# The 1e-9 of a softmax, stored behind its probabilities and summed with them

## The chip, the cores and the metric

One core of a Trainium2 chip runs the kernel. The metric is the device time of one execution in microseconds (us). The kernel before takes 829.16 us, the median of three runs (829.06 to 829.52).

A core has five engines with a queue of instructions each, worked off in order: TensorE (PE in the profile; PEld is its loading of weights), VectorE (DVE), ScalarE (ACT), GpSimd (POOL) and SyncE (SP), which here issues nearly all DMAs. Semaphores order the engines among each other.

## The reference

A windowed attention feeds a gated network; all values are float32.

```python
# q, k, v: (8, 8, 576, 64); heads 0-3 see the last 32 positions,
# heads 4-7 every fourth of the last 128
scores = scale * np.matmul(q, k.transpose(0, 1, 3, 2))
scores = np.where(masks[None, :, :, :], scores, -1000000000.0)
scores = scores - np.max(scores, axis=-1, keepdims=True)
attn = np.exp(scores)
attn = attn / (np.sum(attn, axis=-1, keepdims=True) + 1e-09)
x = np.matmul(attn, v)      # -> 4608 tokens of 512 columns
h = x @ w_in                # 512 x 2048
g = h * (1.0 / (1.0 + np.exp(-1.702 * h)))
out = g @ w_out             # 2048 x 512
```

The change touches the 1e-9 of the division.

## The kernel before

**Attention.** Heads are taken in pairs, four pairs for each of the eight batches: 32 pairs, k = 0 to 31. The queries of a pair lie on the 128 partitions in `QT` = 5 tiles for each of the two heads, and each query has a window of `W` = 64 keys, so the probabilities of a pair are a tile `pr` of 128 x (2 x 5 x 64), 640 columns. For each pair these steps follow one another:

- TensorE makes the scores in PSUM (L470 for the mask, where it is added by a product, and L482). From pair 8 on VectorE adds the mask as it copies them to `pr` (`add_mask`).
- `exponentials`: VectorE takes the maximum of each query (L502), subtracts it (L349), and ScalarE takes the exponential in place (L506).
- `softmax`: VectorE sums the 64 probabilities of each query into `sm`, 128 x 10 (L520). `inverse` adds 1e-9 to the ten sums (L510) and takes the reciprocal (L512). GpSimd, or VectorE, multiplies each head's probabilities by it (L349).
- VectorE transposes blocks of 32 x 32 into `ct` (L529 for the first four pairs, L533 for the others). From pair 4 on, eight copies carry the blocks into `bt` (DMAs for pairs 4 to 7, ScalarE or VectorE after that). TensorE multiplies with v (L575, L607), and `drain_x` copies the result out of PSUM; the copies of the last 64 tokens of a batch (its rests) are steps of their own.

The pairs use two sets of `pr`, `mx`, `sm`, `ct` in turn; pairs 8 to 23 use three. The third `pr` and `ct` lie in units 13 to 15 of a large tile `arena` (`third`), where the q, k and v of pair 3 have lain. Pair 8 is the first that uses it.

**The network.** The weights come as float32 and are split into a high and a low part (`decode`), and each product is the sum of three. Three groups of 512 tokens are done plainly (`Group`, L848 up and L785 to L789 down, `acc_m`). Six more groups are done in blocks p, q, r of two, with seven sums and differences in place of eight products (`Block`, L991 and L1106). While the first weights come in, the four first pairs run alone: this head lasts until about 38 us. Their drains feed the first group's products. The gate (L856, L857 or L1012, L1013) lies between the up and the down products. The attention of later batches is done beside the products of earlier groups. In the head, TensorE also runs products without use (L1237, `idle`).

**The order of the work** is not written out by hand. Each step is handed to `add` with the engines that may do it and its cost in us on each, an urgency, and the names that it reads and writes. A negative cost marks a VectorE step that holds the port which it shares with GpSimd. `Plan.ordered` places all steps one by one, four times over, with the costs as durations, and the queues are then filled in that order. A step that names what another writes comes after it in the plan. So whatever changes a cost or a name can move other steps too, on every engine, and the number of `idle` products as well.

Of the kernel before, what the change touches and what calls it, by code (L numbers as in the profile page):

```python
# [7 lines left out]
F32 = mybir.dt.float32  # L8
F32R = mybir.dt.float32r
AX = mybir.AxisListType  # L10
AF = mybir.ActivationFunctionType
ALU = mybir.AluOpType
# [5 lines left out]
P = 128  # L18
NC = DM // P
NF = DF // P  # L20
GT = 512
# [12 lines left out]
QT = 5  # L34
W = 64
# [7 lines left out]
PE, ACT, DVE, POOL, DMA = range(5)  # L43
# [4 lines left out]
class Plan:  # L48
# [9 lines left out]
    def add(self, costs, urgency, work, reads=(), writes=(), slack=0.0, count=0):  # L58

        i, after = len(self.ops), set()
        for k in reads:
            after.add(self.writer.get(k))
        for k in writes:  # L70
            after.add(self.writer.get(k))
            after.update(self.readers.get(k, ()))
        for k in writes:
            self.writer[k], self.readers[k] = i, []
        for k in reads:
            if k not in writes:
                self.readers.setdefault(k, []).append(i)
        self.ops.append((costs, (urgency, i), work, after - {None, i}, slack, count))
# [138 lines left out]
def tile_windowed_attention_then_gated_mlp(  # L217
# [10 lines left out]
    V, A, G, T = nc.vector, nc.scalar, nc.gpsimd, nc.tensor  # L228
# [8 lines left out]
    add = plan.add  # L237

    def fixed(shape, dt, name):
        return one.tile(shape, dt, tag=name, name=name)  # L240
# [25 lines left out]
    def area(first, n):  # L266
        return arena[:, first:first + n].rearrange("p u n -> p (u n)")
# [13 lines left out]
    sums_o = dram.tile([7 * PAIRS // 2, P, 2 * DM], F32, tag="sums_o", name="sums_o")  # L281
    tokens_x = dram.tile([B * NC, P, GT], F32, tag="tokens_x", name="tokens_x")
    tokens_r = dram.tile([NC, P, B * LT], F32, tag="tokens_r", name="tokens_r")
    prs = [fixed([P, 2, QT, W], F32, f"pr{j}") for j in range(2)]
    mxs = [fixed([P, 2, QT], F32, f"mx{j}") for j in range(3)]
    sms = [fixed([P, 2, QT], F32, f"sm{j}") for j in range(3)]

    cts = [fixed([P, 2, QT, 2, 32], F32, f"ct{j}") for j in range(2)]

    third = area(13, 3)  # L290
    prs.append(third[:, 0:2 * QT * W].rearrange("p (a t w) -> p a t w", a=2, t=QT))
    cts.append(third[:, 2 * QT * W:4 * QT * W].rearrange("p (h t a q) -> p h t a q", h=2, a=2, t=QT))

    four = tc.tile_pool(name="four", bufs=1, space=bass.MemoryType.PSUM)
    first_x = four.__enter__().tile([P, NC, GT], F32, tag="x", name="first_x")
# [9 lines left out]
    ident = fixed([P, P], BF16, "ident")  # L305
    ones = fixed([P, 32], F32, "ones")
    V.memset(ones, 1.0)
    V.memset(ident, 1.0)
    G.affine_select(out=ident, in_=ident, pattern=[[1, P]], compare_op=ALU.is_equal, fill=0.0, base=0,
                    channel_multiplier=-1)  # L310
# [37 lines left out]
    def pair(e, dst, a, b, op):  # L348
        (V if e == DVE else G).tensor_tensor(out=dst, in0=a, in1=b, op=op)  # L349
# [103 lines left out]
    def dilated(k):  # L453
        return k % NC >= NC // 2

    def turn(k):
        return k % (3 if FIRST * NC <= k < INNER else 2)

    def masked(k):

        return k < FIRST * NC
# [31 lines left out]
    def exponentials(k, urgency):  # L493
        u, y = pairs[k], turn(k)
        pr, mx = prs[y], mxs[y]
        PR, MX = f"pr{y}", f"mx{y}"
        held = ("sp",) if masked(k) else ()

        def sp():
            return u["all"] if masked(k) else pr  # L500

        add({DVE: 0.80}, urgency, lambda e: V.tensor_reduce(out=mx, in_=sp(), axis=AX.X, op=ALU.max),  # L502
            held or (PR,), (MX,))
        add({DVE: 0.80 if masked(k) else -0.80}, urgency, lambda e: pair(
            e, pr, sp(), mx[:, :, :, None].broadcast_to([P, 2, QT, W]), ALU.subtract), (*held, MX), (PR,))
        add({ACT: 0.75}, urgency, lambda e: A.activation(prs[y], prs[y], AF.Exp, scale=0.125), (), (PR,))  # L506

    def inverse(k, urgency):
        sm, SM = sms[turn(k)], f"sm{turn(k)}"
        add({DVE: -0.15}, urgency, lambda e: V.tensor_scalar(  # L510
            out=sm, in0=sm, scalar1=1.0e-9, scalar2=None, op0=ALU.add), (), (SM,))
        add({DVE: 0.19}, urgency, lambda e: V.reciprocal(out=sm, in_=sm), (), (SM,))  # L512

    def softmax(k, urgency):

        y = turn(k)
        pr, sm, ct = prs[y], sms[y], cts[y]
        PR, SM, CT = (f"{n}{y}" for n in ("pr", "sm", "ct"))
        exponentials(k, urgency)
        add({DVE: 0.80}, urgency, lambda e: V.tensor_reduce(out=sm, in_=pr, axis=AX.X, op=ALU.add), (PR,), (SM,))  # L520
        inverse(k, urgency)
        for a in range(2):
            add({POOL: 0.85, DVE: -0.48}, urgency, lambda e, a=a: pair(
                e, pr[:, a], pr[:, a], sm[:, a, :, None].broadcast_to([P, QT, W]), ALU.mult), (SM,), (f"{PR}.{a}",))
        if k < NC:

            for a in range(2):
                to = ct.rearrange("p h t a q -> p (h t a q)")[:, a * QT * W:a * QT * W + QT * W]
                add({DVE: 0.48}, urgency, lambda e, a=a, to=to: V.transpose(  # L529
                    out=to, in_=pr[:, a].rearrange("p t w -> p (t w)")), (PR, f"{PR}.{a}"), (f"{CT}.{a}",))  # L530
            return
        for half in (0, 1):
            add({DVE: 0.42}, urgency, lambda e, half=half: V.transpose(  # L533
                out=ct[:, half].rearrange("p t a q -> p a t q"), in_=pr[:, :, :, 32 - 32 * half:64 - 32 * half]),
                (PR, f"{PR}.0", f"{PR}.1"), (f"{CT}.{half}",))

        for m in range(8):
            j, prev = m % 4, m // 4  # L540
            odd, upper = j % 2, j // 2
            row = D * upper + 32 * (odd != prev)
            col = 32 * odd if not prev or odd else 64
            shift = prev and not odd
            tiles = slice(1 if shift and not upper else 0, QT - upper)
            to = slice(1, QT) if upper and not shift else slice(0, tiles.stop - tiles.start)
            dst = bt[row:row + 32, to, :, col:col + 32]
            src = ct[32 * j:32 * j + 32, prev, tiles]

            def work(e, dst=dst, src=src):  # L550
                if e == DMA:
                    load(dst, src)
                else:
                    copy(e, dst, src)

            costs = {DMA: 82} if k < FIRST * NC else {ACT: 0.49, DVE: -0.33}
            add(costs, urgency, work, (f"{CT}.{prev}",), (f"bt.{m}",))
# [134 lines left out]
    def attention(k, urgency):  # L692

        def alone(j):
            add({PE: 1.6 if masked(j) else 1.1}, urgency - 1.0e5, lambda e: scores(j),
                (lots(j)[0], *(["mask"] if dilated(j) else [])), ("sp", "left", f"scores{j}"), 1.0)
            if not masked(j):
                add_mask(j, urgency)

        n = following(k)  # L700
        if k == NC:
            load_qk(k)
            alone(k)
        load_v(k)
        if n and n > k + 1:
            if k == FIRST * NC:
                for j in range(k + 1, n):
                    load_qk(j)
                    alone(j)
            load_qk(n)  # L710
        elif n and k != INNER:
            load_qk(n)
        softmax(k, urgency)
        joint = n is not None and n > k + 1
        if n and not joint and k != INNER:
            alone(n)

        def work(e):
            if joint:
                scores(n)  # L720
            product(k)

        need = [lots(n)[0] if joint else f"scores{n}"] if n else []
        places = ("sp",) if k >= INNER else ("left", "av", "sp") if joint else ("left", "av")
        add({PE: 1.95 if joint else 1.05}, urgency - 1.0e5, work,
            (lots(k)[1], *(f"bt.{m}" for m in range(8)), *need), places, 1.0)
        if joint:
            add_mask(n, urgency)
        drain_x(k, urgency)
# [9 lines left out]
    def unit(i):  # L739
        if i < NU:  # L740
            return arena[:, i]
        if i >= NU + 4:
            n = i - NU - 4
            if n < 4:
                tag = ("qk", "v")[n // 2]
                if f"{tag}_units" not in misc:
                    misc[f"{tag}_units"] = temp([P, 2, GT], F32, tag, f"{tag}_units")
                return misc[f"{tag}_units"][:, n % 2]
            if n >= 8:
                return bt_all[:, GT * (n - 8):GT * (n - 7)]  # L750
            if n < 6:
                return prs[n - 4].rearrange("p a t w -> p (a t w)")[:, 0:GT]
            return cts[n - 6].rearrange("p h t a q -> p (h t a q)")[:, 0:GT]
        if "wi_last" not in misc:
            misc["wi_last"] = temp([P, 4, GT], F32, "wi_last", "wi_last_units")
        return misc["wi_last"][:, i - NU]
# [535 lines left out]
```

## Time and profile before

| | |
|---|---|
| median of 3 runs | 829.16 us |
| profiled execution | 828.89 us |
| its span, from the first to the last instruction | 827.2 us |
| mean granted clock of TensorE | 0.991 |
| TensorE busy | 811.2 us |
| VectorE busy | 669.7 us |
| ScalarE busy | 515.0 us |
| GpSimd busy | 327.8 us |

The profile shows one execution. A row of a group of instructions gives line, engine, operation, what is written and read, the shapes and the count, then the busy time in us and the mean of one in ns, then how long the engine stood idle just before them and on what it waited. A row of the chain gives a start and a duration in us: the chain is followed back from the last instruction, at each step to what released it. A row of the order in time gives start, duration, engine and line, and in brackets an idle time before it. Durations of neighbours overlap a little, because an instruction's end is written down after the next one has begun. `L349` and `L342` are helpers, so their tiles tell which step they are.

### The profile page before, as it was taken

What the parts mean: (1) busy time and instruction counts of PE and PEld (TensorE: products, weight loads), DVE (VectorE), ACT (ScalarE), POOL (GpSimd) and SP (SyncE); (2) the same over time, 40 slices, a digit from 0 to 9 for tenths busy, and PEclk for the clock granted to TensorE, in tenths of its full rate; (3) what the DMA queues carried; (4) which work ended last, traced back from release to release, by engine and by line L of the source; (5) the groups of instructions that cost most, each with busy time, mean ns of one, the idle gap of its engine ahead of it and who ended that gap; (6) DMA issues with size and microseconds to landing.
All of it is one profiled execution on the core that took longest, in us unless ns stands there. A gap on an engine that the chain in (4) does not pass through costs nothing.

```text
span 827.2 us, 18837 instructions
## 1 busy us (share of the span) xinstructions
PE 811.2 (98%) x7240; PEld 653.5 (79%) x7240; DVE 669.7 (81%) x1104; ACT 515.0 (62%) x992; POOL 327.8 (40%) x296
## 2 busy tenths in 40 slices
PE   7899999999999999999999999999999999999997
PEld 4678777888878888878788788888888888888886
DVE  6898989787888778898989998977679876867575
ACT  7998986676676777586776655446446544544340
POOL 3343336566655663324235357331125431112251
PEclk8799999999999999999999999999999999999999
DMA  9476658889757567868878878675665658664546
GB/s 359 152 244 193 181 192 287 295 281 314 249 189 254 183 200 257 267 190 280 279 229 261 261 233 260 219 269 168 214 193 182 211 186 273 203 222 149 189 151 181
DMA packets 109610, 188.12 MB, mean 227 GB/s; under 512 B 26448, under 2 KB 55376, under 8 KB 109520
## 3 DMA queue, kind: packets, MB, share of 16 engines
q1 hardware_dynamic: 109376, 186.78, 69.3%
q8 instruction: 57, 0.93, 0.5%
q14 instruction: 33, 0.27, 0.1%
q10 hardware_dynamic: 144, 0.13, 0.0%
HBM read 140.64 MB, written 45.09 MB: 225 GB/s over the span
## 4 chain that ended last, share of the span: by engine, by line
PE 88%; DVE 7%; ACT 1%; issue 1%; DMA 1%; SPq 0%; DVEq 0%; ACTq 0%
PE hp_m L848 15%; PE up_q L991 9%; PE up_r L991 9%; PE up_p L991 8%; PE second_q_Q L1106 5%; PE second_r_Q L1106 5%; PE second_p_Q L1106 5%; PE acc_m L785 5%; PE acc_m L789 5%; PE acc_m L786 4%; PE sp L482 3%; PE second_r_Z L1106 3%; PE second_R L1106 3%; PE second_q_Z L1106 3%; PE second_p_Z L1106 2%; PE av L607 2%
## 5 line engine op out<-in xcount | busy, mean ns | idle before, releaser
L349 POOL TENSOR_TENSOR arena<-arena 128x256 f32<-128x256 f32 (+3 forms) x109 | 118.0, 1091 | 155.7 <-DVE wi_last_units L349 34.7
L848 PE MATMUL hp_m<-xs,wi_kept 128*128 128x512 f32 x504 | 129.1, 398 | 0.7 <-DVE xs L349 0.4
L848 PEld LDWEIGHTS hp_m<-xs,wi_kept 128*128 128x128 f32 x504 | 93.3, 188 | 22.5 <-DVE arena L857 1.6
L342 ACT ACTIVATE wo_kept<-arena 128x512 fp32r<-128x512 f32 x115 | 71.9, 629 | 42.3 <-PE second_r_Q L1106 11.4
L349 POOL TENSOR_TENSOR wo_kept<-arena,wo_kept 128x512 fp32r<-128x512 f32 x34 | 45.3, 1340 | 105.5 <-ACT wo_kept L342 72.2
L991 PE MATMUL up_p<-wi_kept,xs 128*128 128x512 f32 x336 | 84.7, 394 | 2.2 <-DVE arena L349 1.3
L991 PE MATMUL up_r<-wi_kept,xs 128*128 128x512 f32 x336 | 85.3, 389 | 0.0
L991 PE MATMUL up_q<-wi_kept,xs 128*128 128x512 f32 x336 | 83.4, 389 | 0.0
L991 PEld LDWEIGHTS up_p<-wi_kept,xs 128*128 128x128 f32 x336 | 62.1, 188 | 16.8 <-DVE arena L349 2.2
L991 PEld LDWEIGHTS up_q<-wi_kept,xs 128*128 128x128 f32 x336 | 63.0, 188 | 13.4 <-DVE arena L1013 0.3
L991 PEld LDWEIGHTS up_r<-wi_kept,xs 128*128 128x128 f32 x336 | 63.1, 188 | 13.1
L349 DVE TENSOR_TENSOR wo_kept<-arena,wo_kept 128x512 fp32r<-128x512 f32 x87 | 65.3, 761 | 5.9 <-ACT wo_kept L342 5.4
L349 POOL TENSOR_TENSOR wo_kept<-wi_last_units,wo_kept 128x512 fp32r<-128x512 f32 x23 | 31.9, 1388 | 84.6 <-ACT wo_kept L342 84.6
L785 PE MATMUL acc_m<-gh,wo_kept 128*128 128x512 f32 x156 | 61.7, 395 | 0.4 <-ACT arena L342 0.3
L786 PE MATMUL acc_m<-gh,wo_kept 128*128 128x512 f32 x156 | 60.9, 390 | 0.0
L349 POOL TENSOR_TENSOR pr<-pr,sm 128x320 f32<-128x320 f32 x52 | 43.3, 850 | 43.0 <-DVE sm L512 29.3
L342 ACT ACTIVATE bt<-ct 32x256 f32<-32x256 f32 (+1 forms) x127 | 55.2, 435 | 3.2 <-DVE ct L533 0.9
L1012 ACT ACTIVATE arena<-arena 128x512 f32<-128x512 f32 x60 | 37.5, 628 | 28.9 <-DVE arena L349 25.1
L349 DVE TENSOR_TENSOR gl<-arena,gh 128x512 fp32r<-128x512 f32 x53 | 44.9, 847 | 9.1 <-PE acc_m L789 6.4
L349 DVE TENSOR_TENSOR arena<-arena 128x512 f32<-128x512 f32 (+1 forms) x68 | 50.4, 747 | 0.4
L1013 DVE SCALAR_TENSOR_TENSOR arena<-arena 128x512 f32<-128x512 f32 x60 | 48.1, 807 | 0.7 <-ACT arena L1012 0.2
L342 ACT ACTIVATE wo_kept<-wi_last_units 128x512 fp32r<-128x512 f32 x47 | 29.6, 629 | 30.0 <-PE second_r_Z L1106 8.9
(261 smaller groups left out, 1826.6 us busy)
## 6 DMA issues: line engine op xcount, KB each, us to landing
xs<-sums SPq DMA_DIRECT2D x168, 256.0 KB, 3.3
out_weights<-sums_o SPq DMA_DIRECT2D x63, 512.0 KB, 3.8
qk<-qk_dram SPq DMA_DIRECT2D x29, 576.0 KB, 5.2
xs<-sums_o SPq DMA_DIRECT2D x21, 512.0 KB, 3.6
v<-vp_dram SPq DMA_DIRECT2D x28, 320.0 KB, 4.4
sums<-arena SPq DMA_DIRECT2D x32, 256.0 KB, 3.6
sums_o<-arena SPq DMA_DIRECT2D x32, 256.0 KB, 3.4
arena<-wi_dram SPq DMA_DIRECT2D x15, 512.0 KB, 4.7
```

Source lines behind the costliest of these rows:

```text
L342: A.activation(dst, src, AF.Copy, scale=scale)
L349: (V if e == DVE else G).tensor_tensor(out=dst, in0=a, in1=b, op=op)
L482: T.matmul(dst[:, w:w + n], u["qk"][rows, at:at + 32], u["qk"][rows, S + first:S + first + n], start=not masked(k), stop=True, tile_positi ...
L607: T.matmul(u["x"][i][rows, at:at + last - first], u["v"][keys, a, m], bt[keys, m, a, first:last], start=(bank_, a) not in begun, stop=True ...
L785: T.matmul(self.acc[j], w[:, 0, cols], high, start=f == 0, stop=False)
L786: T.matmul(self.acc[j], w[:, 1, cols], high, start=False, stop=False)
L789: T.matmul(self.acc[j], w[:, 0, P * j:P * j + P], low, start=False, stop=f == NF - 1)
L848: T.matmul(hps[f], wi(f)[:, st, cols], mv[:, c], start=c == 0 and k == 0, stop=c == NC - 1 and k == 2)
L991: T.matmul(self.banks[place], xs[:, slot, at:at + P], wi_kept[:, 2 * a + c, mv], start=fresh and c == 0 and k == 0, stop=c == 1 and k == 2 ...
L1012: add({ACT: 0.60}, -10.0, lambda e: A.activation(unit(tmp), src(), AF.Tanh, scale=0.851), need, own(tmp))
L1013: add({DVE: -0.70 if need[0][0] == "A" else 0.70}, -10.0, lambda e: V.scalar_tensor_tensor(out=unit(dst), in0=unit(tmp), scalar=1.0, in1=s ...
L1106: T.matmul(self.second[key], w[:, st, cols], mv, start=fresh and y == 0 and k == 0, stop=y == 1 and k == 2, skip_group_check=True)
```

## The change

Each `pr` becomes a set of 128 x (2 x 5 x 65): behind the 64 probabilities of a query stands one more column that holds 1e-9. The sum reads all 65, and the addition of L510 goes. The steps that work on probabilities use a view of the first 64 columns of each row, whose rows then begin 65 words apart. Two sets get their column by a memset ahead of the plan, on VectorE; the third gets it by a step of the plan, on VectorE or GpSimd, which names `pr2`, `first v3` and `first qk3`. The names `first v3` and `first qk3` are written by the loads of pair 3 and also by the rests of batch 1 (pairs 4 to 7). The third `ct` lies ten words further on.

```diff
-    prs = [fixed([P, 2, QT, W], F32, f"pr{j}") for j in range(2)]
+    sets = [fixed([P, 2, QT, W + 1], F32, f"pr{j}") for j in range(2)]
...
-    prs.append(third[:, 0:2 * QT * W].rearrange("p (a t w) -> p a t w", a=2, t=QT))
-    cts.append(third[:, 2 * QT * W:4 * QT * W].rearrange("p (h t a q) -> p h t a q", h=2, a=2, t=QT))
+    sets.append(third[:, 0:2 * QT * (W + 1)].rearrange("p (a t w) -> p a t w", a=2, t=QT))
+    prs = [p[:, :, :, 0:W] for p in sets]
+    cts.append(third[:, 2 * QT * (W + 1):2 * QT * (2 * W + 1)].rearrange("p (h t a q) -> p h t a q", h=2, a=2, t=QT))
...
     V.memset(ones, 1.0)
+    for p in sets[0:2]:
+        V.memset(p[:, :, :, W], 1.0e-9)
     V.memset(ident, 1.0)
...
     def inverse(k, urgency):
         sm, SM = sms[turn(k)], f"sm{turn(k)}"
-        add({DVE: -0.15}, urgency, lambda e: V.tensor_scalar(
-            out=sm, in0=sm, scalar1=1.0e-9, scalar2=None, op0=ALU.add), (), (SM,))
         add({DVE: 0.19}, urgency, lambda e: V.reciprocal(out=sm, in_=sm), (), (SM,))
...
-        add({DVE: 0.80}, urgency, lambda e: V.tensor_reduce(out=sm, in_=pr, axis=AX.X, op=ALU.add), (PR,), (SM,))
+        add({DVE: 0.81}, urgency, lambda e: V.tensor_reduce(out=sm, in_=sets[y], axis=AX.X, op=ALU.add), (PR,), (SM,))
...
                 add({DVE: 0.48}, urgency, lambda e, a=a, to=to: V.transpose(
-                    out=to, in_=pr[:, a].rearrange("p t w -> p (t w)")), (PR, f"{PR}.{a}"), (f"{CT}.{a}",))
+                    out=to.rearrange("p (t w) -> p t w", w=W), in_=pr[:, a]), (PR, f"{PR}.{a}"), (f"{CT}.{a}",))
...
             if k == FIRST * NC:
+                add({DVE: 0.10, POOL: 0.10}, urgency, lambda e: (V if e == DVE else G).memset(sets[2][:, :, :, W], 1.0e-9),
+                    (), ("pr2", "first v3", "first qk3"))
```

The blocks use the sets as plain storage once the attention is done; they take the first 512 columns of a set in place of a `pr`.

More of the change, by code (lines that the diff above doesn't have):

```diff
@@ L751, in unit @@
             if n < 6:
-                return prs[n - 4].rearrange("p a t w -> p (a t w)")[:, 0:GT]
+                return sets[n - 4].rearrange("p a t w -> p (a t w)")[:, 0:GT]
             return cts[n - 6].rearrange("p h t a q -> p (h t a q)")[:, 0:GT]
```

## The prediction

> **What bounds the kernel now.** I read the page first, then the stretches of the span, then the chain of work that ended last, then the groups of instructions with shapes kept apart, and last the order in time around the touched steps. The page:
>
> ```profile
> span 827.2 us, 18837 instructions
> PE 811.2 (98%) x7240; PEld 653.5 (79%) x7240; DVE 669.7 (81%) x1104; ACT 515.0 (62%) x992; POOL 327.8 (40%) x296
> PE 88%; DVE 7%; ACT 1%; issue 1%; DMA 1%; SPq 0%; DVEq 0%; ACTq 0%
> ```
>
> TensorE is busy for 98% of the span, and the chain lies on it for 88%. VectorE, the engine that the change relieves, carries 7% of the chain, some 58 us. The stretches say where a faster VectorE could matter (columns: busy time and instruction count of PE, PEld, DVE, ACT, POOL, then granted clock, DMA share, GB/s):
>
> ```profile
> 0.00:40.00 40.00, 32.12 (x844) 20.68 (x845) 29.32 (x67) 32.85 (x48) 14.90 (x23) 0.83 0.68 252
> ...
> 90.00:122.00 32.00, 31.91 (x352) 24.97 (x352) 28.61 (x50) 28.58 (x53) 11.03 (x9) 1.00 0.60 189
> 122.00:150.00 28.00, 27.56 (x360) 21.37 (x359) 24.90 (x44) 17.43 (x39) 18.89 (x19) 1.00 0.84 274
> 150.00:800.00 650.00, 647.16 (x5089) 528.24 (x5088) 525.12 (x844) 387.67 (x776) 257.78 (x226) 1.00 0.71 229
> 800.00:827.20 27.20, 22.41 (x99) 18.21 (x98) 16.28 (x26) 4.10 (x7) 7.08 (x5) 0.96 0.57 174
> ```
>
> TensorE stands idle for 7.88 us in the first 40 us (40.00 less 32.12), for 4.79 us after 800, and between 90 and 800 for only 0.09 + 0.44 + 2.84 = 3.37 us. The last reciprocal of a softmax starts at 451.7:
>
> ```profile
> L512 DVE RECIPROCAL sm<-sm x32: 198/210/219, 12.0 to 451.7; 128x10 f32<-128x10 f32 x32
> ```
>
> so the tail has none of this work. Whatever VectorE is spared, the middle can return at most 3.4 us, and the rest must come from the head.
>
> **The change part by part.** The times stand against the profiled execution, 828.89 us for a span of 827.2; the median of the timed runs is 829.16, 0.03% above it.
>
> *The removed addition.* There are 32 of them, one per pair of heads:
>
> ```profile
> L510 DVE TENSOR_SCALAR sm<-sm 128x10 f32<-128x10 f32 x32 | 7.9, 247 | 0.4
> L520 DVE TENSOR_REDUCE sm<-pr 128x10 f32<-128x640 f32 x26 | 21.0, 808 | 2.2 <-ACT pr L506 2.0
> L533 DVE STREAM_TRANSPOSE ct<-pr 128x320 f32<-128x320 f32 x44 | 20.5, 491 | 0.5 <-POOL pr L349 0.5
> ```
>
> They take 7.9 us of VectorE's 669.7, 1.2%. The chain of work says how much of that sets the end. It holds the addition three times:
>
> ```profile
> 9.83 0.82 DVE sm L520
> ...
> 11.24 0.09 DVE sm L510
> ...
> 133.20 0.08 DVE sm L510
> ...
> 141.94 0.17 DVE sm L510
> ...
> 167.96 0.73 DVE sm L520
> ```
>
> That is 0.09 + 0.08 + 0.17 = 0.34 us to win. The other 29 additions lie beside TensorE's work. The Trainium skill has its own price in "Perfetto Trace Analysis", section "Optimizing Scalar/DVE Operations": about 60 ns of engine time for each VectorE instruction on SBUF, and three of those would make 0.18 us in place of 0.34. The row's mean of 247 ns is four times that; I go by the chain.
>
> *The longer sum.* Each reduction reads 650 elements in place of 640. From the two rows above, an element costs (808 - 491) / (640 - 320) = 1.0 ns, as an estimate that takes both operations to be streams of the same rate; so each sum grows by 0.01 us, 0.3 us over all 32. The chain holds five sums between 9.83 and 167.96, so 0.05 us is lost.
>
> *The two memsets at the start* stand on VectorE between the one of the ones and the one of the identity:
>
> ```profile
> 0.88 0.09 DVE L307 MEMSET ones<- 128x32 f32 x1 [0.88 <-PEq L1282]
> 0.94 0.17 DVE L308 MEMSET ident<- 128x128 bf16 x1
> 4.22 0.69 PE L470 MATMUL sp<-plain,ident 128*128 128x320 bf16 x2 [1.64 <-DVE plain L328]
> 5.07 1.44 PE L482 MATMUL sp<-qk 64*32 64x64 f32 x84 [0.15 <-DMA qk<-qk_dram]
> ```
>
> One memset of this size holds the engine for 0.94 - 0.88 = 0.06 us, so the identity, GpSimd's selections behind it and the first mask come 0.12 us later. The first mask product at 4.22 waits for that, but the scores behind it wait another 0.15 us for q and k to land: 0.12 fits, so I take nothing. Without that cover it costs 0.12 us.
>
> *The reciprocal comes sooner.* With the addition gone, the reciprocal follows the sum, and the multiplication on GpSimd follows that. Where it could matter most is the last pair of the head (k = 3), whose product and split let the full-rate matmuls begin:
>
> ```profile
> 28.12 1.20 DVE L510 TENSOR_SCALAR sm<-sm 128x10 f32<-128x10 f32 x1
> 29.35 0.22 DVE L512 RECIPROCAL sm<-sm 128x10 f32<-128x10 f32 x1
> ...
> 31.80 0.27 DVE L344 COPY arena<-first_x 128x64 f32<-128x64 f32 x1 [1.68 <-ACT xs L342]
> 31.94 0.50 DVE L529 STREAM_TRANSPOSE ct<-pr 128x320 f32<-128x320 f32 x1
> ...
> 33.31 0.51 DVE L529 STREAM_TRANSPOSE ct<-pr 128x320 f32<-128x320 f32 x1
> ```
>
> ```profile
> 28.01 1.28 POOL L349 TENSOR_TENSOR wi_kept<-arena,wi_kept 128x512 fp32r<-128x512 f32 x1 [0.40 <-ACT wi_kept L342]
> 29.65 1.73 POOL L349 TENSOR_TENSOR pr<-pr,sm 128x320 f32<-128x320 f32 x2 [0.36 <-DVE sm L512]
> ```
>
> The addition took 1.20 us there where those of the chain above show 0.08 to 0.17: it stood until GpSimd's operation of 28.01 ended at 29.29. The reciprocal can start 1.23 us sooner, but GpSimd itself is taken until 29.29, so its multiplication gains 0.36 us. And in the present order the transposes stand behind the copy at 31.80, which waits for ScalarE and not for the softmax. So the gain is between 0 and 1.23 us; with the order unchanged it is 0, and I take that, because the copy's row has 1.68 us of waiting to swallow it.
>
> *The new wait.* The third set lies where the v and q, k of the pair k = 3 lay. Its memset, a planned step on VectorE or GpSimd, names "first v3", which the copies of the last 64 tokens of pair 7 write, and "pr2", which the maximum of pair 8 reads. So pair 8's maximum must now follow pair 7's drain, which it did not:
>
> ```profile
> 112.42 0.82 DVE L502 TENSOR_REDUCE mx<-arena 128x10 f32<-128x640 f32 x1
> ...
> 114.21 0.81 DVE L349 TENSOR_TENSOR arena<-arena,mx 128x640 f32<-128x640 f32 x1
> ...
> 122.68 0.42 DVE L398 TENSOR_SCALAR arena<-arena 128x512 uint32<-128x512 uint32 x1
> 123.91 0.69 DVE L857 SCALAR_TENSOR_TENSOR arena<-arena,hp_m 128x512 f32<-128x512 f32 x1 [0.81 <-ACT arena L856]
> 124.51 0.81 DVE L520 TENSOR_REDUCE sm<-arena 128x10 f32<-128x640 f32 x1
> ```
>
> ```profile
> 120.18 0.73 ACT L506 ACTIVATE arena<-arena 128x640 f32<-128x640 f32 x1
> ...
> 122.16 0.47 ACT L342 ACTIVATE arena<-sp 128x16 f32<-128x16 f32 x2
> ```
>
> ```profile
> 105.00:124.50 19.50, 19.50 (x192) 15.50 (x192) 15.45 (x28) 16.28 (x40) 7.45 (x7) 1.00 0.51 172
> 124.50:143.50 19.00, 18.56 (x215) 14.05 (x213) 18.15 (x32) 11.37 (x22) 11.48 (x11) 1.00 0.87 288
> ```
>
> The drain's two small copies end at 122.16 + 0.47 = 122.63. The maximum moves from 112.42 to 122.7 or later, the subtraction and the exponential after it: 0.82 + 0.81 = 1.63 us of VectorE leave a stretch with 4.05 us free (19.50 less 15.45) for one with 0.85 (19.00 less 18.15). If the memset stands on VectorE, the gate's operation at 123.91 is queued behind it, and TensorE's next products wait for that. Between nothing and 0.82 + 0.81 + 0.73 (exponential) + 0.10 (two of the memset rows) = 2.46 us. I take nothing: 0.81 us of idle before 123.91 holds the maximum, the 0.85 us hold the subtraction, and pair 8's rest (its addition is the one of the chain at 133.20, 8 us behind the sum of 124.51) is not in a hurry.
>
> *The order of everything else.* The steps' order is planned from costs, and 32 costs go, 32 change, one comes. What TensorE stands idle for in the middle, 3.37 us, bounds what a luckier order gives; I take as much for an unluckier one, and zero as the value, since nothing in the trace favours a side.
>
> Sum: 828.89 - 0.34 + 0.05 = **828.6 us**. The measurement of this kernel can tell about 0.2%, 1.66 us, from no change, so this is no change.
>
> **The rivals.** *The head gets shorter.* If the planner, free of the addition, puts pair 3's multiplication ahead of GpSimd's operation at 28.01 and its transposes ahead of the copy at 31.80, the whole 1.23 us is won: 828.6 - 1.23 = 827.4, faster by 0.2%; half of the middle's 3.37 us on top gives 825.7. For it: the 1.20 us of an operation over ten columns. Against it: the copy at 31.80.
>
> *Pair 8's wait reaches TensorE.* If VectorE stands at pair 8's sum until the late exponential is done, the gate's operations queue behind it and all 2.46 us count: 828.6 + 2.46 = 831.1, slower by 0.23%. It decides when 2.2 of the 2.46 us become TensorE's wait (830.8). For it: VectorE is busy for 18.15 of the 19.00 us into which the work moves. Against it: the 8 us that the softmax now waits behind its sum.
>
> *Rows of 65 words make each pass over the probabilities slower.* Every second row of 64 then begins on an odd word. Head pairs pass over them by maximum, subtraction and two transposes, 0.82 + 0.81 + 2 x 0.49 = 2.61 us; the other operations scale alike. If these lose a fifth, four head pairs cost 4 x 0.52 = 2.1 us and 32 pairs 16.7 us of VectorE, 8.8 more than the 7.9 removed, of which the chain's 7% is 0.6: 831.3. At a tenth it is 828.6 + 1.04 + 0.03 = 829.7, no change; the point is a sixth, 830.8. No row here has such a stride. The Trainium skill, "Vector Engine (DVE) Microarchitecture Reference", section 5.2, measures 1.30 ns in place of 1.054 per column for pairs of words that start odd; on half the rows that would be some 12% and a time of 830.0, an estimate from that page, which speaks of short pairs and not of runs of 64.
>
> *An unluckier order* costs up to 3.37 us: 832.0.
>
> **How the numbers follow.** The forecast gets 0.42, since the chain holds little of what goes. The shorter head gets 0.32: the head has the most idle time, and a planner with fewer steps to place there may well use it. Pair 8's wait gets 0.13 for its slack, odd rows 0.05, since a sixth is more than even the page's price, and an unluckier order 0.08. Hence faster 0.32, same 0.42, slower 0.26. The range reaches half-way into the outer cases: 825.8, next to the rival with a better middle, to 831.4, past pair 8's price and short of the unluckiest order.
>
> **What would show it.** The additions are gone, and sums take 0.01 us more each; memsets of 128x10 stand near 0.9 us and the first scores still start near 5.07. The maximum of pair 8 starts after 122 and TensorE's idle time from 122 to 150 stays near 0.44 us. The full-rate matmuls start within 0.3 us of now, where the chain shows them from 38.18 on:
>
> ```profile
> 38.18 3.92 PE hp_m L848 x16
> ```
>
>  VectorE's passes over the probabilities keep 0.81 us. The forecast is wrong if TensorE's idle time in the first 40 us falls by more than a microsecond, if that of 122 to 150 grows by as much, or if those passes grow.

## The result, and the profile after

The changed kernel takes 834.2 us, the median of six runs (832.22 to 835.32), against 829.14 us before (six runs, 828.83 to 829.65): a ratio of 1.0056, with a 95% interval from 1.0042 to 1.0070. It is slower, by 4.6 us in the means and 5.1 us in the medians, and outside the stated range of 825.8 to 831.4. The profiled execution took 833.98 us.

The page of the changed kernel shows nothing of this at first sight: the busy times of all engines stand within some 1% of those before. In the chain, DMAs carry 4% and not 1%, but e5 below, which is faster than before, has 4% as well.

```profile
span 832.2 us, 18826 instructions
PE 811.9 (98%) x7245; PEld 654.5 (79%) x7245; DVE 669.9 (80%) x1088; ACT 513.7 (62%) x982; POOL 323.7 (39%) x293
PE 85%; DVE 7%; DMA 4%; issue 1%; ACT 1%; SPq 0%; DVEq 0%; ACTq 0%
```

The stretches show where the 5.0 us of span came from. First the kernel before, with the stretch from 40 to 90 that the prediction left out and its long stretch cut in three, then the changed kernel (columns as there):

```profile
40.00:90.00 50.00, 50.00 (x503) 40.07 (x502) 45.46 (x79) 44.41 (x76) 18.11 (x15) 1.00 0.69 217
...
150.00:345.00 195.00, 194.72 (x2494) 157.72 (x2493) 161.03 (x283) 137.04 (x310) 105.67 (x111) 1.00 0.76 251
345.00:500.00 155.00, 152.75 (x1278) 123.23 (x1277) 138.18 (x228) 104.18 (x220) 58.67 (x49) 1.00 0.77 245
500.00:800.00 300.00, 299.68 (x1320) 247.29 (x1319) 225.90 (x335) 146.46 (x248) 93.44 (x67) 1.00 0.64 206
```

```profile
0.00:40.00 40.00, 31.02 (x840) 19.62 (x840) 28.87 (x61) 28.53 (x45) 16.34 (x24) 0.83 0.64 242
40.00:90.00 50.00, 47.73 (x461) 37.45 (x463) 45.65 (x82) 44.94 (x73) 13.23 (x13) 1.00 0.72 230
...
122.00:150.00 28.00, 27.58 (x296) 22.22 (x295) 25.45 (x41) 18.75 (x41) 17.32 (x16) 1.00 0.66 219
150.00:345.00 195.00, 194.12 (x2601) 157.70 (x2599) 157.15 (x273) 134.92 (x300) 107.03 (x114) 1.00 0.75 247
345.00:500.00 155.00, 153.42 (x1279) 123.29 (x1278) 138.86 (x224) 106.11 (x221) 60.51 (x48) 1.00 0.78 255
500.00:800.00 300.00, 298.58 (x1314) 245.98 (x1313) 230.02 (x335) 146.66 (x249) 90.24 (x64) 1.00 0.64 205
```

TensorE's idle time (length less busy time) went from 0.00 to 2.27 us between 40 and 90, from 0.28 to 0.88, from 2.25 to 1.58 and from 0.32 to 1.42 in the last three. Together that is 3.3 of the 5.0 us. The greatest piece lies right behind the head, where before there was none. In the first 40 us idle time is no measure of a loss, because TensorE also runs products without use there: it went from 7.88 to 8.98 us, but in e1 below, which takes the time of before, it is 9.40.

The work that is left tells how far a kernel has come. Behind 90 us TensorE is busy for another 811.16 - 32.12 - 50.00 = 729.04 us before, and for 811.90 - 31.02 - 47.73 = 733.15 us in the changed kernel. So 4.1 of the 5.0 us are lost by 90 us. This measure is rough: e1 and e3 below, whose orders are that of before until about 112 us, have 0.5 and 1.6 us more left than before.

The head itself ends later. The order in time on TensorE in the changed kernel, from the second part of the second head pair's product (k = 1, at 22.21) to the product of the last (k = 3, at 38.19):

```profile
22.21 1.61 PE L577 MATMUL first_x<-ct,arena 32*64 32x32 f32 x87 [2.21 <-issue]
23.75 0.71 PE L474 MATMUL sp<-arena,ident 128*128 128x320 bf16 x2
...
38.19 1.08 PE L577 MATMUL first_x<-ct,arena 32*64 32x64 f32 x80
39.20 5.08 PE L852 MATMUL hp_m<-xs,wi_kept 128*128 128x512 f32 x21
45.51 1.66 PE L852 MATMUL hp_m<-xs,wi_kept 128*128 128x512 f32 x6 [1.24 <-DVE arena L861]
47.01 0.39 PE L789 MATMUL acc_m<-gh,wo_kept 128*128 128x512 f32 x1
```

and before:

```profile
19.62 0.71 PE L470 MATMUL sp<-arena,ident 128*128 128x320 bf16 x2 [0.23 <-DVE pr L349]
...
34.00 1.08 PE L575 MATMUL first_x<-ct,arena 32*64 32x64 f32 x80
...
38.18 3.92 PE L848 MATMUL hp_m<-xs,wi_kept 128*128 128x512 f32 x16 [0.43 <-DVE xs L349]
41.94 0.39 PE L785 MATMUL acc_m<-gh,wo_kept 128*128 128x512 f32 x1
```

Before, the last pair's scores (their mask product) start at 19.62, ahead of the second pair's product; now they start at 23.75, behind it, and that product had stood still for 2.21 us in the middle ("issue": nothing that the profile shows held it). The last pair's own product starts at 38.19 and not at 34.00, and the first down product (`acc_m`) at 47.01 and not at 41.94. Not all of those 5.1 us are lost, since more up products stand ahead of it.

On VectorE the two orders part before that. The changed kernel, with one row of GpSimd at its head:

```profile
10.51 1.28 POOL L353 TENSOR_TENSOR wi_kept<-arena,wi_kept 128x512 fp32r<-128x512 f32 x1 [5.51 <-ACT wi_kept L346]
...
9.94 0.83 DVE L522 TENSOR_REDUCE sm<-pr 128x10 f32<-128x650 f32 x1 [0.20 <-ACT pr L510]
10.81 0.22 DVE L514 RECIPROCAL sm<-sm 128x10 f32<-128x10 f32 x1
10.94 0.76 DVE L506 TENSOR_REDUCE mx<-sp 128x10 f32<-128x640 f32 x1
11.94 1.12 DVE L394 TENSOR_SCALAR arena<-arena 128x512 uint16<-128x512 uint16 x1 [0.23 <-ACT arena L399]
12.87 0.84 DVE L353 TENSOR_TENSOR pr<-sp,mx 128x640 f32<-128x640 f32 x1
```

and before:

```profile
10.56 0.68 DVE L349 TENSOR_TENSOR wi_kept<-arena,wi_kept 128x512 fp32r<-128x512 f32 x1
11.16 0.17 DVE L510 TENSOR_SCALAR sm<-sm 128x10 f32<-128x10 f32 x1
11.24 0.82 DVE L502 TENSOR_REDUCE mx<-sp 128x10 f32<-128x640 f32 x1
11.97 0.21 DVE L512 RECIPROCAL sm<-sm 128x10 f32<-128x10 f32 x1
12.09 0.82 DVE L349 TENSOR_TENSOR pr<-sp,mx 128x640 f32<-128x640 f32 x1
```

The first reciprocal does come sooner, at 10.81 in place of 11.97, and the second pair's maximum too. That is the new order and not the missing addition: a step of the weights' decoding (`wi_kept`, 0.68 us at 10.56) has gone from VectorE to GpSimd, and in e1, without the addition and in the old order, the first reciprocal starts at 11.94. The planner then puts another step of the decoding (L394, 1.12 us and an idle 0.23) ahead of the second pair's subtraction, which so moves from 12.09 to 12.87. From there the orders differ throughout the head; which of the differences makes the last pair late was not separated.

### The profile page after: what moved, and what is told of

Its sections match the earlier page's. It is cut to its first block, busy times and chain, and to the rows that moved or that the text cites. A ratio compares the mean times of both kernels' runs of the same rounds, so it can differ in the third digit from the quotient of the medians.

```text
span 832.2 us, 18826 instructions
## 1 busy us (share of the span) xinstructions
PE 811.9 (98%) x7245; PEld 654.5 (79%) x7245; DVE 669.9 (80%) x1088; ACT 513.7 (62%) x982; POOL 323.7 (39%) x293
## 4 chain that ended last, share of the span: by engine, by line
PE 85%; DVE 7%; DMA 4%; issue 1%; ACT 1%; SPq 0%; DVEq 0%; ACTq 0%
PE hp_m L852 15%; PE up_r L995 9%; PE up_p L995 8%; PE up_q L995 7%; PE second_q_Q L1110 5%; PE second_r_Q L1110 5%; PE acc_m L793 5%; PE acc_m L789 5%; PE acc_m L790 5%; PE second_p_Q L1110 3%; PE sp L486 3%; PE second_r_Z L1110 3%; PE second_q_Z L1110 3%; PE second_R L1110 3%; PE av L609 2%; PE second_p_Z L1110 2%
## 5 line engine op out<-in xcount | busy, mean ns | idle before, releaser
L353 POOL TENSOR_TENSOR arena<-arena 128x256 f32<-128x256 f32 (+3 forms) x102 | 108.4, 1077 | 151.0 <-ACT arena L346 29.0
L353 POOL TENSOR_TENSOR wo_kept<-arena,wo_kept 128x512 fp32r<-128x512 f32 x36 | 49.3, 1376 | 113.9 <-ACT wo_kept L346 91.0
L353 DVE TENSOR_TENSOR wo_kept<-arena,wo_kept 128x512 fp32r<-128x512 f32 x85 | 67.0, 797 | 5.6 <-ACT wo_kept L346 5.0
L353 DVE TENSOR_TENSOR arena<-arena 128x512 f32<-128x512 f32 (+1 forms) x71 | 54.5, 772 | 1.6 <-ACT arena L346 1.0
L353 DVE TENSOR_TENSOR gl<-arena,gh 128x512 fp32r<-128x512 f32 x53 | 40.4, 761 | 9.3 <-PE acc_m L793 6.1
L860 ACT ACTIVATE arena<-hp_m 128x512 f32<-128x512 f32 x48 | 28.7, 599 | 29.0 <-PE hp_m L852 20.7
```

Source lines behind the costliest of these rows:

```text
L860: add({ACT: 0.60}, -10.0, lambda e: A.activation(g32, hps[f], AF.Tanh, scale=0.851), (place,), ("g32",))
```

## The experiments

Each ratio is to executions of the kernel before that were made beside the experiment. "Order" is the order in which the planner fills the queues of instructions; the planner also chooses the engine of a step that several may do, so a new order can also move work from one engine to another.

**e1: the new instructions in the old order.** Against the changed kernel:

```diff
+        add({DVE: -0.15}, urgency, lambda e: None, (), (SM,))
         add({DVE: 0.19}, urgency, lambda e: V.reciprocal(out=sm, in_=sm), (), (SM,))
...
-        add({DVE: 0.81}, urgency, lambda e: V.tensor_reduce(out=sm, in_=sets[y], ...
+        add({DVE: 0.80}, urgency, lambda e: V.tensor_reduce(out=sm, in_=sets[y], ...
...
-                add({DVE: 0.10, POOL: 0.10}, urgency, lambda e: (V if e == DVE else G).memset(...
+            if k == FIRST * NC:
+                V.memset(sets[2][:, :, :, W], 1.0e-9)
```

The empty step keeps the planned cost of the addition that is gone; the third memset is issued inside the step of pair 8's maximum and has none of its own.

> The change's instructions in the order of before: 65 columns, no addition, three memsets, while the planner still counts a step of 0.15 us for each addition (which issues nothing), 0.80 us for the sum, and no step for the third memset, which is issued with the maximum of pair 8. Theory A, that the loss is the new order of the steps: 828 to 829.5 us, no slower than before, as the prediction's sum had it. Theory B, that the instructions themselves cost it (rows 65 words apart, the memsets at the start, the longer sums): 832 to 835 us.

Measured: 828.97 us, ratio 0.9996 (0.9987 to 1.0005). In its trace VectorE, ScalarE and GpSimd run the steps of before in the sequence of before, the additions and memsets aside. Theory B falls: the 65 columns, the memsets, the longer sums and the missing addition come to nothing together, within -1.1 and +0.4 us.

**e2: the old instructions in the new order.** Against the kernel before:

```diff
-        add({DVE: -0.15}, urgency, lambda e: V.tensor_scalar(
-            out=sm, in0=sm, scalar1=1.0e-9, scalar2=None, op0=ALU.add), (), (SM,))
-        add({DVE: 0.19}, urgency, lambda e: V.reciprocal(out=sm, in_=sm), (), (SM,))
+        def both(e):
+            V.tensor_scalar(out=sm, in0=sm, scalar1=1.0e-9, scalar2=None, op0=ALU.add)
+            V.reciprocal(out=sm, in_=sm)
+
+        add({DVE: 0.19}, urgency, both, (), (SM,))
```

with 0.81 for the sum and an empty step for the third memset.

> The instructions of before, the additions among them, in the order that the changed kernel's planner makes: the addition is issued together with the reciprocal behind it, the sum is planned with 0.81 us, and a step that issues nothing stands for the third memset. Theory A (order): 833 to 835.5 us. Theory B (instructions): 828.5 to 830 us.

Measured: 833.38 us, ratio 1.0043 (1.0028 to 1.0057). The loss comes with the order, without one new instruction: VectorE, ScalarE and GpSimd run their steps in the sequence of the changed kernel, the additions and memsets aside. Its stretches have the mark of the changed kernel, idle time between 40 and 90:

```profile
0.00:40.00 40.00, 31.12 (x844) 19.11 (x845) 30.59 (x63) 29.38 (x45) 16.80 (x24) 0.91 0.65 242
40.00:90.00 50.00, 48.06 (x490) 37.42 (x489) 46.05 (x87) 45.69 (x73) 13.74 (x13) 1.00 0.73 227
```

while e1 has that of the kernel before:

```profile
40.00:90.00 50.00, 50.00 (x503) 40.05 (x502) 45.19 (x76) 44.35 (x73) 18.11 (x15) 1.00 0.70 222
```

**e3: only the third memset's step is new in the plan**; the addition's 0.15 and the sum's 0.80 are counted as in e1.

> The changed kernel, but the planner counts the addition's 0.15 us and 0.80 us for the sum as before, so its order is that of before until pair 8, where the third memset's step with its three names makes the maximum of pair 8 wait for pair 7's drain. Theory A with the loss in the head: 828 to 830 us, the head as before. Theory C, that pair 8's wait costs most of it: 831 us or more, with TensorE idle for over 2 us between 122 and 150.

Measured: 835.03 us, ratio 1.0071 (1.0054 to 1.0089), the slowest of all. This was not expected by the theory that puts the loss in the head: the head is that of before. Theory C has the time right, past its 831 us, but not the place. TensorE is idle for 1.91 us between 122 and 150, a little less than its 2 us and 1.5 more than before. More comes later, in stretches with other work: 0.8, 0.9 and 1.2 us more idle time than before between 150 and 345, 345 and 500, and 500 and 800. The first and the last two of these stretches:

```profile
122.00:150.00 28.00, 26.09 (x357) 20.49 (x354) 24.07 (x39) 16.08 (x35) 15.61 (x17) 1.00 0.81 273
...
345.00:500.00 155.00, 151.84 (x1265) 121.88 (x1264) 135.90 (x214) 107.16 (x224) 61.16 (x46) 0.99 0.76 241
500.00:800.00 300.00, 298.46 (x1316) 246.63 (x1315) 226.66 (x334) 145.77 (x247) 92.12 (x65) 1.00 0.64 206
```

**e4: the kernel before, with the sum planned as 0.81 in place of 0.80.**

```diff
-        add({DVE: 0.80}, urgency, lambda e: V.tensor_reduce(out=sm, in_=pr, axis=AX.X, op=ALU.add), (PR,), (SM,))
+        add({DVE: 0.81}, urgency, lambda e: V.tensor_reduce(out=sm, in_=pr, axis=AX.X, op=ALU.add), (PR,), (SM,))
```

> The kernel before with one number changed in the plan: the sum is planned with 0.81 in place of 0.80 us. Each instruction is that of before; only their order can differ. Theory A: the time moves by more than 1 us either way, since a hundredth in the plan is enough for another order. Theories B and C: within 0.5 us of before.

Measured: 830.01 us, ratio 1.0014 (1.0002 to 1.0026). Slower by 0.9 us from a hundredth of a microsecond in the plan, a little less than the 1 us expected.

**e5: the changed kernel, planned as before for the first four pairs.**

```diff
+        if k < NC:
+            add({DVE: -0.15}, urgency, lambda e: None, (), (SM,))
         add({DVE: 0.19}, urgency, lambda e: V.reciprocal(out=sm, in_=sm), (), (SM,))
...
-        add({DVE: 0.81}, urgency, lambda e: V.tensor_reduce(out=sm, in_=sets[y], ...
+        add({DVE: 0.80 if k < NC else 0.81}, urgency, lambda e: V.tensor_reduce(out=sm, in_=sets[y], ...
```

> The changed kernel, but for the first four pairs the planner counts the addition's step and 0.80 us as before, so the order is that of before to about 70 us and goes its own way after that. Theory A1, that the reordered head costs most of the loss: 828.5 to 830.5 us, with TensorE never idle from 40 to 90 us. Theory A2, that the later order loses just as much: 832 us or more.

Measured: 826.96 us, ratio 0.9971 (0.9960 to 0.9982): faster than the changed kernel by 7 us and faster than before. That is below what theory A1 gave, so the order behind the head is a luckier one as well. In the trace it parts from that of before at about 52 us and not at 70. TensorE does stand idle between 40 and 90, for 0.74 us (in an execution of 829.84 us, the slowest of nine):

```profile
40.00:90.00 50.00, 49.26 (x486) 39.12 (x488) 44.58 (x78) 42.92 (x70) 14.82 (x12) 1.00 0.69 210
```

Pair 8 waits for pair 7 in the plan of this kernel too, and it is faster than before all the same.

**e6: the changed kernel without the third memset's step** (issued as in e1).

> The changed kernel without the third memset's step in the plan (it is issued with the maximum of pair 8): the order is that of the changed kernel to about 120 us, and pair 8 no longer waits for pair 7. Theory A1 (head): 832 to 834.5 us, with 2 us of idle TensorE between 40 and 90 as in the changed kernel. Theory C (pair 8's wait): 829.5 to 831 us.

Measured: 832.89 us, ratio 1.0039 (1.0027 to 1.0051), as theory A1 had it. The head is that of the changed kernel, and so is the idle time behind it:

```profile
0.00:40.00 40.00, 30.91 (x842) 19.60 (x843) 29.64 (x61) 29.08 (x45) 16.66 (x24) 0.87 0.64 242
40.00:90.00 50.00, 48.43 (x493) 37.78 (x492) 44.94 (x84) 45.49 (x73) 13.96 (x13) 1.00 0.72 233
```

**e7: only the addition's step is dropped from the plan** (0.80 for the sum, the third memset as in e1).

> The instructions of the change, with the addition's step gone from the plan and nothing else changed there: 0.80 us for the sum, no step for the third memset. Theory A: another order again, so a time that neither the changed kernel nor the one before has; between 828 and 836 us, with a head unlike that of before. If dropping the step is what makes the bad head: TensorE idle for over 1 us between 40 and 90.

Measured: 828.43 us, ratio 0.9990 (0.9979 to 1.0001), idle for 0.05 us between 40 and 90. Dropping the step alone does not make the bad head; here it takes the hundredth for the sum as well.

**e8: the kernel before, with the addition planned as 0.14 in place of 0.15.**

> The instructions of before; the planner counts 0.14 in place of 0.15 us for the addition. Theory A: another order and a time that differs from before by 0.5 us or more, likely slower, since the order of before stands at the low end of the orders seen so far (829.1 against 830.0, 833.4, 834.2 and 835.0). If small numbers don't matter: 829 us within 0.3.

Measured: 832.73 us, ratio 1.0038 (1.0025 to 1.0051), 2.61 us idle between 40 and 90. Every instruction is one of before.

**e9: the changed kernel, with the sum planned as 0.80 in place of 0.81.**

> The changed kernel with one number of the plan changed: the sum is counted with 0.80 in place of 0.81 us. Its head is then that of the run in which only the step was dropped, which had a good one. Theory A with the head as the main cost: 828 to 831 us, TensorE idle for less than 0.5 us between 40 and 90. If the dropped step or the memset's step as such were the cause: 833 to 835 us as in the changed kernel.

Measured: 830.8 us, ratio 1.0019 (1.0009 to 1.0029), idle for 0.05 us between 40 and 90. One number of the plan, and no instruction, takes the ratio from 1.0056 to 1.0019, some 3 us.

**e10, e11, e12: three more orders of the new instructions.** As e1, with 0.05, 0.10 and 0.20 us counted for the addition that is no longer there:

```diff
-        add({DVE: -0.15}, urgency, lambda e: None, (), (SM,))
+        add({DVE: -0.10}, urgency, lambda e: None, (), (SM,))
```

> The change's instructions; the plan counts 0.05 us for the addition that is no longer issued, 0.80 us for the sum, no step for the third memset. One more draw of the order. Theory A: anywhere between 827 and 836 us; where it lands follows from TensorE's idle time between 40 and 90 and from 345 to 650. If the order mattered little: 829 us within 0.5.

Measured: 830.75 us, ratio 1.0019 (1.0010 to 1.0028).

> As the run with 0.05 us, with 0.10 us: one more draw. Theory A: anywhere between 827 and 836 us. If the order mattered little: 829 us within 0.5.

Measured: 826.74 us, ratio 0.9972 (0.9960 to 0.9984), just below the 827 us that were expected at the least. With e5 the fastest; its idle times are low all the way:

```profile
40.00:90.00 50.00, 49.83 (x508) 39.08 (x511) 46.15 (x80) 46.43 (x78) 13.96 (x12) 1.00 0.73 236
...
150.00:345.00 195.00, 195.00 (x2498) 158.47 (x2497) 163.75 (x281) 135.54 (x303) 96.81 (x104) 1.00 0.77 252
345.00:500.00 155.00, 153.99 (x1284) 124.54 (x1283) 135.81 (x217) 103.51 (x213) 71.65 (x56) 1.00 0.77 247
```

> As the run with 0.05 us, with 0.20 us: one more draw, whose order is that of before to about 70 us. Theory A with the head as the main cost: 827 to 831 us, below most of the draws with another head.

Measured: 830.33 us, ratio 1.0013 (1.0005 to 1.0022). That is as expected, though in the trace its order parts from that of before at about 58 us and not at 70.

Side by side, sorted by ratio. The idle times are those of TensorE in one profiled execution each, length less busy time of the stretch; its time is given too, since it can lie off the median (e5's is its slowest of nine, e7's its fastest of twelve). The last column is the work that TensorE has left at 90 us, less that of before, in us:

| kernel | instructions | ratio | profiled, us | idle 40-90 | 122-150 | 150-345 | 345-500 | 500-800 | left at 90 |
| --- | --- | --- | --- | --- | --- | --- | --- | --- | --- |
| e5 | new | 0.9971 | 829.84 | 0.74 | 0.01 | 1.50 | 1.71 | 0.13 | +0.81 |
| e11 | new | 0.9972 | 825.76 | 0.17 | 0.52 | 0.00 | 1.01 | 0.35 | -2.20 |
| e7 | new | 0.9990 | 826.57 | 0.05 | 0.57 | 0.93 | 0.47 | 0.51 | -1.43 |
| e1, order of before | new | 0.9996 | 828.97 | 0.00 | 0.33 | 0.13 | 2.25 | 0.16 | +0.47 |
| before | old | 1 | 828.89 | 0.00 | 0.44 | 0.28 | 2.25 | 0.32 | 0 |
| e12 | new | 1.0013 | 829.90 | 0.00 | 1.08 | 0.38 | 0.71 | 0.61 | +0.67 |
| e4 | old | 1.0014 | 829.88 | 0.00 | 1.50 | 0.73 | 1.50 | 0.25 | +0.25 |
| e9 | new | 1.0019 | 829.41 | 0.05 | 0.65 | 1.49 | 1.24 | 0.00 | +0.39 |
| e10 | new | 1.0019 | 832.42 | 0.35 | 0.00 | 1.77 | 1.66 | 1.79 | +0.65 |
| e8 | old | 1.0038 | 834.26 | 2.61 | 0.09 | 0.60 | 2.44 | 0.10 | +5.50 |
| e6 | new | 1.0039 | 832.00 | 1.57 | 0.28 | 0.54 | 1.01 | 0.42 | +3.47 |
| e2, order of the changed kernel | old | 1.0043 | 833.38 | 1.94 | 0.00 | 1.49 | 1.32 | 1.34 | +3.72 |
| the changed kernel | new | 1.0056 | 833.98 | 2.27 | 0.42 | 0.88 | 1.58 | 1.42 | +4.11 |
| e3 | new | 1.0071 | 834.98 | 0.00 | 1.91 | 1.11 | 3.16 | 1.54 | +1.62 |

Twelve orders stand here. Apart from that of before, three of the eleven others are faster (e7's interval reaches 1.0001), eight are slower, and the middle one is 0.2% slower. Where two kernels share an order, they share the time: e1 and before, e2 and the changed kernel. All four kernels with over 1.5 us of idle time between 40 and 90 take 1.0038 or more. These four (e8, e6, e2 and the changed kernel) also have 3.5 to 5.5 us more work left at 90 us, most or all of what their profiled executions are longer by. Two kernels lose behind 90 us instead: the profiled executions of e3 and e10 are 6.1 and 3.5 us longer than that of before, with only 1.62 and 0.65 us more left at 90.

Pairs of kernels that differ in one entry of the plan say what moves the time. The third memset's step makes it longer each time: e1 to e3 (0.9996 to 1.0071), e7 to e9 (0.9990 to 1.0019) and e6 to the changed kernel (1.0039 to 1.0056). So does the hundredth for the sum: before to e4 (1 to 1.0014), e7 to e6 (0.9990 to 1.0039) and e9 to the changed kernel (1.0019 to 1.0056). Dropping the addition's step goes both ways: e1 to e7 (0.9996 to 0.9990) and e3 to e9 (1.0071 to 1.0019), but e4, whose instructions are the old ones, to e6 (1.0014 to 1.0039). One and the same entry costs 1.4 to 6.2 us, or 1.2 to 4.1, by what stands beside it. Whether the first two have a cost of their own, or whether six draws fell on the slow side by chance, is not shown; e5 has both behind its head and is fast.

## Why the prediction was wrong

The step that failed is the last of its parts: "What TensorE stands idle for in the middle, 3.37 us, bounds what a luckier order gives; I take as much for an unluckier one, and zero as the value, since nothing in the trace favours a side." The new order cost 0.43% by itself, 3.6 us (e2, ratio 1.0043), and 4.6 us in the changed kernel itself, more than even the 3.37 us of the unluckier order. The step was off in three ways.

- *The bound.* It took the idle time of the middle and left the head out. An order can lose in the head too: the last pair's scores moved from 19.62 to 23.75, and 2.27 us went idle right behind the head. The rival on the head looked at one sign only, a head that gets shorter. Of the signs that were named, the full-rate matmuls within 0.3 us of now (38.18) failed: their long run starts at 39.20.
- *The value.* Zero is not the middle. The order of before lies at the good end of those tried: the eleven others, which are variants of one plan and no random draws, range from 0.29% faster to 0.71% slower, with 0.19% slower in the middle. Its page could have hinted at it, with 3.37 us of idle time in 710 us; an order with so little idle time, one may argue, has more room above it than below.
- *The chance.* The unluckier order got 0.08, as the last of four rivals, while the sum was made with care for terms of 0.05 and 0.34 us that no run can tell from nothing.

The rest of the sum was right where it could be seen by itself, in e1. The ratio of 0.9996 holds the predicted 0.29 us of gain and also none; no run settles it. The head of e1 went as the part on the reciprocal said, on VectorE:

```profile
27.86 0.20 DVE L519 RECIPROCAL sm<-sm 128x10 f32<-128x10 f32 x1
...
31.80 0.28 DVE L348 COPY arena<-first_x 128x64 f32<-128x64 f32 x1 [2.23 <-ACT xs L346]
31.94 0.51 DVE L536 STREAM_TRANSPOSE ct<-pr 128x320 f32<-128x320 f32 x1
```

and on GpSimd:

```profile
28.99 1.84 POOL L353 TENSOR_TENSOR pr<-pr,sm 128x320 f32<-128x320 f32 x2
```

The reciprocal starts 1.49 us sooner than before (27.86 for 29.35), the multiplication 0.66 us sooner (28.99 for 29.65, where 0.36 us were worked out), and the transposes stand behind the copy at 31.80 as they did. The gain went into that copy's wait, which grew from 1.68 to 2.23 us. So this saving ended as idle time in front of something else; where the other additions' time went was not followed.

The two memsets hold back the identity by 0.04 us in the changed kernel, a third of the 0.12 estimated, and the scores' wait covers it:

```profile
0.92 0.09 DVE L311 MEMSET pr<- 128x10 f32 x2
0.98 0.17 DVE L312 MEMSET ident<- 128x128 bf16 x1
```

The longer sum takes 819 ns in place of 808, the 0.01 us of the working. Most passes over rows 65 words apart take what they took: the exponential 740 ns as before, the maximum 812 (809 before), the transposes 491 as before. The subtraction rose from 950 to 1008 ns, but it took 1021 with the old rows in the new order (e2) and 963 with the new rows in the old order (e1); six more subtractions, on `arena`, take 894 to 1160 ns in the kernels with old rows and 894 to 1172 in those with new ones. So that goes with the order for the most part. With e1 at the time of before, that rival is out.

```profile
L522 DVE TENSOR_REDUCE sm<-pr 128x10 f32<-128x650 f32 x26 | 21.3, 819 | 2.2 <-ACT pr L510 1.9
L535 DVE STREAM_TRANSPOSE ct<-pr 128x320 f32<-128x320 f32 x44 | 20.6, 491 | 0.0
L510 ACT ACTIVATE pr<-pr 128x640 f32<-128x640 f32 x26 | 19.2, 740 | 3.1 <-DVE pr L353 2.6
L353 DVE TENSOR_TENSOR pr<-pr,mx 128x640 f32<-128x640 f32 x18 | 18.1, 1008 | 0.1
L506 DVE TENSOR_REDUCE mx<-pr 128x10 f32<-128x640 f32 x18 | 14.6, 812 | 0.4
```

and the subtraction before:

```profile
L349 DVE TENSOR_TENSOR pr<-pr,mx 128x640 f32<-128x640 f32 x18 | 17.1, 950 | 0.0
```

The Trainium skill's price for pairs of words that start odd ("Vector Engine (DVE) Microarchitecture Reference", section 5.2) does not carry over to runs of 64 words, by these rows.

Pair 8's maximum moved as described, but no engine waited for the memset. In the changed kernel the memset stands on GpSimd and the maximum on VectorE:

```profile
120.49 0.11 POOL L709 MEMSET arena<- 128x10 f32 x1
...
128.45 0.81 DVE L506 TENSOR_REDUCE mx<-arena 128x10 f32<-128x640 f32 x1
```

The memset is done before pair 7's copies out of PSUM begin (at 124.56 on ScalarE), and 7.9 us before the maximum. So the wait exists in the plan alone, and what moves the maximum is its place in VectorE's queue. TensorE's idle time between 122 and 150 is 0.42 us, as before (0.44): the later maximum was hidden there, as forecast. But its step is one more thing that changes the order of all that follows. The prediction took nothing for it; in the three pairs above it cost 1.4 to 6.2 us, alone it gave e3, the slowest kernel, and together with other costs it is part of e5, one of the two fastest.

What stays open: the changed kernel's loss lies ahead of 90 us for the most part, by the work left there, but how much of it comes from the late last pair and how much from the rest of the order until then was not separated. The head of before under the same later costs (e5) and the changed head under other later costs (e6) both speak for the head, with 0.9971 and 1.0039; but in each of them the later order differs as well, and e3 loses 6 us with the head of before. Why the planner, whose costs are close to the rows, ranks these orders as it does was not tried.

## What to carry to other kernels

In a kernel whose order comes from a planner, an edit is two edits: the instructions, and a new draw of the order. Measure them apart, by keeping the old plan's steps and costs with the new instructions and the other way round; here the first was worth nothing that could be measured and the second cost 0.4%. Before costing a small saving to a tenth of a microsecond, ask how far orders of equal merit lie apart, by moving one planned cost by a hundredth: if that spread is greater than the saving, the spread is the forecast. Here drawing a few orders and timing them (e5, e11: 0.3% faster than before) was worth more than the edit.

## What the runs showed that was not expected

- Nearly the same work in eleven new orders took from 826.7 to 835.0 us in the median, while TensorE's busy share of the span stayed between 97 and 98%.
- Waits that the profile puts down to "issue" stay where they are, and the order decides which instruction they hit. Counted in TensorE's recorded instructions, weight loads included, they stand ahead of the 706th, the 962nd and the 1218th in all fourteen kernels, 256 apart, at about 16, 22 and 26 us (in e7, e8 and e9 ahead of the 1474th too). Before the change they took 1.76, 1.60 and 0.90 us; after it, 0.89, 2.21 and 0.39 us. The second one held the last pair's scores before and the second pair's product after. A supply of instructions in blocks of 256 would look like this, but no run here tests it; and e9 and e11, with 3.1 and 3.0 us at the second, are not among the slow kernels.
- Single executions of one kernel lie up to some 5 us apart: 5.4 us from the fastest to the slowest of twelve in e4, 4.8 us of nine in e5 and 3.1 us of six in the changed kernel. The kernel before shows 0.8 us over the six beside the changed kernel, but 3.8 us over the 32 beside e9 to e12. So a difference of 1 us needs many executions, and one trace alone can mislead. Why they differ was not tried.
